# Norm sums and inverse norms of the next batch: fp32 matmuls replaced by sums of three bf16 parts

## Chip, cores, metric

One core of one Trainium2 chip. The metric is the device time of one execution in microseconds (us), the median of several. A ratio always compares with runs of the kernel before on the same chip and in the same rounds, whose medians lay between 823.33 and 823.57 us in the experiments. In a profile PE is TensorE (PEld its weight loads), DVE VectorE, ACT ScalarE, POOL GpSimd.

## The reference

Two stages: cross-covariance attention in four batches, then a gated feed-forward block over all rows.

```python
qn = q / (np.linalg.norm(q, axis=1, keepdims=True) + 1e-06)      # q, k, v: 4 x 6016 x 256
kn = k / (np.linalg.norm(k, axis=1, keepdims=True) + 1e-06)
s = kn.transpose(0, 2, 1) @ qn / tau                             # 256 x 256 per batch
a = softmax(s)                                                   # over the last axis (written out in the original)
x = v @ a
out = (silu(x @ w_gate) * (x @ w_val)) @ w_out                   # d_ff = 1536
```

## The kernel before

It never forms x. For each batch it multiplies the softmax into the two weight matrices (here Wg and Wv), then streams the values in chunks of up to 512 rows, 12 steps a chunk, 144 steps a batch. A step is two matmuls into `g_ps`, two into `v_ps`, four into `o_new` for the chunk before. While the chunks of batch b run, a plan slips the norms, logits, softmax and weight products of batch b+1 between the steps. The first batch has its own code. The change touches the plan and the norm part:

```python
def gv_step(b, ci, f, sv):                    # one step; psum_gv has two buffers per tag
    ...
    nc.scalar.activation(silu[:, :mv], g_ps[:, :mv], ACT.Silu)
    nc.vector.tensor_mul(sv[:, f, :mv], silu[:, :mv], v_ps[:, :mv])     # frees v_ps

def norm_acc(b, t):                           # squares of one pair of row groups
    ...
    for which in range(2):
        nc.scalar.activation(sq[:, :pm, which, :], ..., ACT.Square)
    ...
    for s in range(pm):
        nc.vector.tensor_add(acc, acc, sq[:, s, :, :])

def norm_cols(b):                             # sums over partitions, one column per 128 channels
    for n in range(2 * CH):
        w, h = divmod(n, CH)
        nc.tensor.matmul(cs[:, n:n + 1], acc[:, w, h * P:(h + 1) * P],
                         ones_f[:, 0:1], start=True, stop=True)          # fp32
    ...                                       # inv = 1 / (sqrt + 1e-6), on GpSimd

def norm_diag(b):
    for h in range(CH):
        nc.vector.tensor_scalar_mul(diag[:, h, :], in0=identf, scalar1=inv[:, CH + h:CH + h + 1])

def norm_rows(b):                             # inverse norms of k along the free axis
    nc.tensor.matmul(ps, ones_f, state[b, "diag"], start=True, stop=True)   # fp32
    nc.vector.tensor_copy(ink, ps)

# OutStage: at every sixth step half of an output chunk is copied out of PSUM,
# by ScalarE at steps 5, 17, 29, ... of a batch, by VectorE at 11, 23, 35, ...

LOAD0, SQ0 = 10, 22
for t in range(NP):                           # NP = 24 pairs
    step = SQ0 + (5 * t) // 2
    plan[step].append((norm_acc, t))
    plan[step + 1].append((gemm1_pair, t))
S1 = SQ0 + (5 * NP) // 2 + 1
plan[S1].append((norm_cols,))
plan[S1 + 6].append((norm_diag,))
plan[S1 + 7].append((norm_rows,))
...
```

Of the kernel before, what the change touches and what calls it, by code (L numbers as in the profile page):

```python
# [8 lines left out]
FP32 = mybir.dt.float32  # L9
BF16 = mybir.dt.bfloat16  # L10
FP8 = mybir.dt.float8e5
ALU = mybir.AluOpType
# [5 lines left out]
def kernel(  # L18
# [11 lines left out]
    nc = tc.nc  # L30
    P = 128

    B, N, C = q.shape
    D, DFF = moe_w_gate.shape
    assert C == D and C == 2 * P
    CH = C // P
# [24 lines left out]
    work = ctx.enter_context(tc.tile_pool(name="work", bufs=2))  # L61
# [13 lines left out]
    ones_bf = const.tile([P, P], BF16)  # L75
    ones_f = const.tile([P, P], FP32)
# [4 lines left out]
    identf = const.tile([P, P], FP32)  # L81
    ident = const.tile([P, P], BF16)
# [11 lines left out]
    state = {}  # L94
# [174 lines left out]
    def norm_acc(b, t):  # L269
# [12 lines left out]
        for s in range(pm):  # L282
            nc.vector.tensor_add(acc, acc, sq[:, s, :, :])  # L283

    def norm_cols(b):

        acc = state[b, "acc"]
        cs = psum_m.tile([P, 2 * CH], FP32, tag="misc")
        for n in range(2 * CH):
            w, h = divmod(n, CH)  # L290
            nc.tensor.matmul(cs[:, n:n + 1], acc[:, w, h * P:(h + 1) * P],  # L291
                             ones_f[:, 0:1], start=True, stop=True)
        inv = work.tile([P, 2 * CH], FP32, tag="inv")
        nc.vector.tensor_copy(inv, cs)  # L294
        nc.gpsimd.tensor_tensor(out=inv, in0=inv, in1=half, op=ALU.pow)  # L295
        nc.gpsimd.tensor_scalar_add(inv, in0=inv, scalar1=1e-6)
        nc.gpsimd.tensor_tensor(out=inv, in0=inv, in1=minus, op=ALU.pow)
        state[b, "inv"] = inv

    def norm_diag(b):  # L300
        inv = state[b, "inv"]
        diag = work.tile([P, CH, P], FP32, tag="diag")
        for h in range(CH):
            nc.vector.tensor_scalar_mul(diag[:, h, :], in0=identf,
                                        scalar1=inv[:, CH + h:CH + h + 1])
        state[b, "diag"] = diag

    def norm_rows(b):
        ps = psum_m.tile([P, C], FP32, tag="misc")
        nc.tensor.matmul(ps, ones_f, state[b, "diag"], start=True, stop=True)  # L310
        ink = work.tile([P, C], FP32, tag="ink")
        nc.vector.tensor_copy(ink, ps)
        state[b, "ink"] = ink
# [130 lines left out]
                    nc.sync.dma_start(out=self.dst[:, j0:j0 + m, :], in_=o_sb[:, :m, :])  # L444


    LOAD0, SQ0 = 10, 22
    plan = [[] for _ in range(STEPS)]
    for g in range(len(groups)):
        plan[LOAD0 + 5 * g].append((load_qk, g, 0))  # L450
# [1 line left out]
    for t in range(NP):  # L452
        step = SQ0 + (5 * t) // 2
        plan[step].append((norm_acc, t))
        plan[step + 1].append((gemm1_pair, t))
    S1 = SQ0 + (5 * NP) // 2 + 1
    plan[S1].append((norm_cols,))
    plan[S1 + 6].append((norm_diag,))
    plan[S1 + 7].append((norm_rows,))
    plan[S1 + 9].append((logits, 0))  # L460
    plan[S1 + 10].append((logits, 1))
    plan[S1 + 11].append((half_tanh,))
    for n in range(4):
        plan[S1 + 14 + n].append((recip, n))
    plan[S1 + 18].append((exponentials,))
    plan[S1 + 20].append((row_sums,))
    for u in range(len(wp_units)):
        plan[S1 + 22 + (u * 3) // 2].append((wp_unit, u))

    def background(b, step):  # L470
        for what, *args in plan[step]:
# [108 lines left out]
```

## Time and profile before

| | before |
|---|---|
| median time, us (5 rounds) | 823.41 (823.39 to 823.59) |
| span of the profiled run, us | 821.8 |
| TensorE busy, share of the span | 97% |
| chain that ended last, share on TensorE | 92% |
| GpSimd busy, us | 90.1 |

The reading goes from the chain (TensorE sets the end) to the timeline of TensorE, where the price of an inserted block is the distance between the `g_ps` starts around it, beyond the 1.30 us of a plain step. Every step time in this document is such a distance. The prediction below shows those lines. One caution on busy time: this trace has 4937 matmul records where the one after has 5039, because some are missing (weight loads: 5024 and 5039, and the change adds 15).

### The profile page before, as it was taken

What the parts mean: (1) busy time and instruction counts of PE and PEld (TensorE: products, weight loads), DVE (VectorE), ACT (ScalarE), POOL (GpSimd) and SP (SyncE); (2) the same over time, 40 slices, a digit from 0 to 9 for tenths busy, and PEclk for the clock granted to TensorE, in tenths of its full rate; (3) what the DMA queues carried; (4) which work ended last, traced back from release to release, by engine and by line L of the source; (5) the groups of instructions that cost most, each with busy time, mean ns of one, the idle gap of its engine ahead of it and who ended that gap; (6) DMA issues with size and microseconds to landing.
All of it is one profiled execution on the core that took longest, in us unless ns stands there. A gap on an engine that the chain in (4) does not pass through costs nothing.

```text
span 821.8 us, 13520 instructions
## 1 busy us (share of the span) xinstructions
PE 800.2 (97%) x4937; PEld 489.6 (60%) x5024; DVE 552.4 (67%) x870; ACT 461.8 (56%) x826; POOL 90.1 (11%) x171
## 2 busy tenths in 40 slices
PE   7799999999999999999999999999999999999998
PEld 4556566665665566565565656666556565666656
DVE  5576888675655888867556688877665555555554
ACT  2566777555445677645545677755544544544543
POOL 5433000133200000024300000013000000000000
PEclk9999999999999999999999999999999999999999
DMA  9999912169942121129991111125912112112101
GB/s 88 145 160 134 135 39 65 39 119 140 144 90 46 39 65 45 47 52 147 143 150 52 46 52 39 40 65 107 166 39 65 45 40 65 52 39 65 49 26 58
DMA packets 92673, 64.57 MB, mean 79 GB/s; under 512 B 52560, under 2 KB 91472, under 8 KB 91856
## 3 DMA queue, kind: packets, MB, share of 16 engines
q0 software_dynamic: 18656, 27.01, 26.0%
q1 hardware_dynamic: 73952, 36.71, 18.4%
q8 instruction: 39, 0.64, 0.3%
q14 instruction: 26, 0.21, 0.1%
HBM read 78.64 MB, written 36.70 MB: 140 GB/s over the span
## 4 chain that ended last, share of the span: by engine, by line
PE 92%; DMA 3%; ACT 2%; DVE 2%; issue 1%; POOL 0%; DVEq 0%; ACTq 0%; POOLq 0%
PE o_new L432 30%; PE v_ps L404 29%; PE g_ps L404 28%; DMA q_sb<-in_q_dram 2%; PE ps L373 2%; PE kq_new L149 2%; ACT sq L274 1%; DVE sv L408 1%; DMA k_sb<-in_k_dram 1%; DVE acc_new L283 1%; PE cs L291 0%; PE ss_new L176 0%; ACT sq L166 0%; ACT silu L407 0%; PE unit_ps L373 0%
## 5 line engine op out<-in xcount | busy, mean ns | idle before, releaser
L408 DVE TENSOR_TENSOR sv<-silu,v_ps 128x512 bf16<-128x512 bf16 (+1 forms) x576 | 382.6, 673 | 220.1 <-ACT silu L407 218.9
L407 ACT ACTIVATE silu<-g_ps 128x512 bf16<-128x512 f32 (+1 forms) x576 | 337.5, 587 | 305.2 <-PE g_ps L404 252.1
L432 PE MATMUL o_new<-w_out_sb,sv 128*128 128x256 bf16 x2256 | 338.4, 273 | 1.5
L404 PE MATMUL v_ps<-vT,Wv 128*128 128x512 bf16 (+1 forms) x1100 | 324.3, 374 | 6.2 <-DVE sv L408 3.5
L404 PE MATMUL g_ps<-vT,Wg 128*128 128x512 bf16 (+1 forms) x1075 | 319.7, 375 | 0.2
L432 PEld LDWEIGHTS <-sv 128*128 128x128 bf16 x2256 | 220.7, 98 | 140.8
L404 PEld LDWEIGHTS <-Wv 128*128 128x128 bf16 x1152 | 112.7, 98 | 135.0 <-issue 5.4
L404 PEld LDWEIGHTS <-Wg 128*128 128x128 bf16 x1152 | 107.1, 98 | 27.6 <-issue 0.2
L283 DVE TENSOR_TENSOR acc_new<-acc_new,sq 128x512 f32<-128x512 f32 x135 | 93.3, 691 | 23.6 <-ACT sq L274 21.2
L274 ACT ACTIVATE sq<-q_sb 128x512 bf16<-128x512 fp8e5 x72 | 44.3, 615 | 0.0
L274 ACT ACTIVATE sq<-k_sb 128x512 bf16<-128x512 fp8e5 x72 | 44.1, 612 | 0.0
L149 PE MATMUL kq_new<-k_sb,q_sb 128*128 128x512 fp8e5 x184 | 43.3, 317 | 0.3 <-DMA k_sb<-in_k_dram 0.3
L295 POOL TENSOR_TENSOR inv<-inv,half 128x4 f32<-128x4 f32 x3 | 3.1, 1035 | 343.9 <-DVE inv L294 343.9
L441 ACT COPY o_sb<-o_new 128x512 f32<-128x512 f32 x48 | 28.1, 585 | 14.0 <-PE o_new L432 13.7
L443 DVE COPY o_sb<-o_new 128x512 f32<-128x512 f32 (+1 forms) x48 | 31.8, 662 | 3.0 <-PE o_new L432 3.0
L104 POOL DMA_DIRECT2D q_sb<-in_q_dram x48 | 26.1, 544 | 40.1 <-DMA q_sb<-in_q_dram 15.1
L104 POOL DMA_DIRECT2D k_sb<-in_k_dram x48 | 25.9, 540 | 39.5 <-DMA q_sb<-in_q_dram 20.8
L112 POOL DMA_DIRECT2D vb<-in_v_dram x47 | 23.6, 505 | 23.3 <-DMA k_sb<-in_k_dram 14.2
L176 PE MATMUL ss_new<-sq,ones_bf 128*128 128x256 bf16 x91 | 18.3, 285 | 7.5 <-DVE sq L163 6.2
L163 DVE TENSOR_TENSOR sq<-k_sb 128x512 bf16<-128x512 fp8e5 (+1 forms) x24 | 15.2, 681 | 14.2 <-DMA k_sb<-in_k_dram 12.5
L166 ACT ACTIVATE sq<-q_sb 128x512 bf16<-128x512 fp8e5 x23 | 13.0, 619 | 20.1 <-DMA q_sb<-in_q_dram 16.6
L149 PEld LDWEIGHTS <-q_sb 128*128 128x256 fp8e5 x184 | 23.1, 140 | 2.0 <-DMA q_sb<-in_q_dram 0.8
(79 smaller groups left out, 164.5 us busy)
## 6 DMA issues: line engine op xcount, KB each, us to landing
out_dram<-o_sb SPq DMA_DIRECT2D x92, 256.0 KB, 2.4
vb<-in_v_dram POOLq DMA_DIRECT2D x43, 256.0 KB, 10.7
k_sb<-in_k_dram POOLq DMA_DIRECT2D x44, 128.0 KB, 11.6
q_sb<-in_q_dram POOLq DMA_DIRECT2D x44, 128.0 KB, 11.8
w_gate_sb<-in_moe_w_gate_dram POOLq DMA_DIRECT2D x3, 256.0 KB, 9.5
w_val_sb<-in_moe_w_val_dram POOLq DMA_DIRECT2D x3, 256.0 KB, 9.6
w_out_sb<-in_moe_w_out_dram POOLq DMA_DIRECT2D x1, 768.0 KB, 14.3
vb<-in_v_dram POOLq DMA_DIRECT2D x4, 192.0 KB, 4.5
```

Source lines behind the costliest of these rows:

```text
L104: nc.gpsimd.dma_start(out=dst[:, gs:gs + gm, :], in_=src[b].rearrange("(p s) c -> p s c", s=NS)[:, gs:gs + gm, :])
L112: nc.gpsimd.dma_start(out=vb[:mv, :].rearrange("(p s) c -> p (s c)", s=cm), in_=v[b, cs * P:cs * P + mv, :].rearrange("(p s) c -> p (s c)" ...
L149: nc.tensor.matmul(kq[:, jh, :], q_sb[:, ps:ps + 2, js], k_sb[:, ps:ps + 2, :], start=(t == 0 and jh == 0), stop=last, perf_mode=DR, skip_ ...
L176: nc.tensor.matmul(state[b, "ss", which], ones_bf, sq[:, s, :], start=(t == 0 and s == 0), stop=(t == t_last and s == pm - 1))
L274: nc.scalar.activation(sq[:, :pm, which, :], qk_tiles[b][which][:, ps:ps + pm, :], ACT.Square)
L283: nc.vector.tensor_add(acc, acc, sq[:, s, :, :])
L404: nc.tensor.matmul(dst[:, :mv], W[:, kk, fs], vT[:, kk, :mv], start=(kk == 0), stop=(kk == CH - 1))
L407: nc.scalar.activation(silu[:, :mv], g_ps[:, :mv], ACT.Silu)
L408: nc.vector.tensor_mul(sv[:, f, :mv], silu[:, :mv], v_ps[:, :mv])
L432: nc.tensor.matmul(self.o_ps[:, j % 2, :], self.sv[:, f, j * P:(j + 1) * P], w_out_sb[:, f, :], start=(f == 0), stop=(f == FH - 1))
L441: nc.scalar.copy(o_sb[:, :m, :], self.o_ps[:, :m, :])
L443: nc.vector.tensor_copy(o_sb[:, :m, :], self.o_ps[:, :m, :])
```

## The change

Intent: no fp32 matmul beside the chunks. A float32 is cut into three bf16 parts whose sum is meant to be exact, the cutting goes to GpSimd, which is mostly idle (11% busy before), and TensorE multiplies the three parts in bf16 and adds them in PSUM. To give GpSimd time, everything behind the squares moves away from them by 10 to 15 steps, and loads and squares move one step earlier, so that on the batch's own count the former are 9 to 14 steps later.

```diff
+    def split3(src, shape, tag):
+        ...
+        nc.gpsimd.tensor_copy(hi, src)
+        nc.gpsimd.tensor_tensor(out=rest, in0=src, in1=hi, op=ALU.subtract)
+        nc.gpsimd.tensor_copy(mid, rest)
+        nc.gpsimd.tensor_tensor(out=lo, in0=rest, in1=mid, op=ALU.subtract)
+        return hi, mid, lo
+
+    def norm_split(b):
+        state[b, "acc3"] = split3(state[b, "acc"], [P, 2, C], "acc")
     def norm_cols(b):
-            nc.tensor.matmul(cs[:, n:n + 1], acc[:, w, h * P:(h + 1) * P],
-                             ones_f[:, 0:1], start=True, stop=True)
+            for i, part in enumerate(state[b, "acc3"]):
+                nc.tensor.matmul(cs[:, n:n + 1], part[:, w, h * P:(h + 1) * P],
+                                 ones_bf[:, 0:1], start=(i == 0), stop=(i == 2))
...
+        parts = split3(inv[:, CH:], [P, CH], "ink")
+        for i, part in enumerate(parts):
+            nc.gpsimd.tensor_copy(scal[:, i, :], part)
     def norm_diag(b):
+        for i in range(3):
+            for h in range(CH):
+                nc.vector.tensor_scalar_mul(diag[:, i, h, :], in0=ident, scalar1=scal[:, i, h:h + 1])
     def norm_rows(b):
-        nc.tensor.matmul(ps, ones_f, state[b, "diag"], start=True, stop=True)
+        for i in range(3):
+            nc.tensor.matmul(ps, ones_bf, state[b, "diag"][:, i], start=(i == 0), stop=(i == 2))
...
-    LOAD0, SQ0 = 10, 22
+    LOAD0, SQ0 = 9, 21
-    plan[S1].append((norm_cols,))
-    plan[S1 + 6].append((norm_diag,))
-    plan[S1 + 7].append((norm_rows,))
+    plan[S1].append((norm_split,))
+    plan[S1 + 10].append((norm_cols,))
+    plan[S1 + 20].append((norm_diag,))
+    plan[S1 + 22].append((norm_rows,))
...                                          # logits to row sums 15 steps later, weight products 14
```

More of the change, by code (lines that the diff above doesn't have):

```diff
@@ L283, in norm_acc @@
             nc.vector.tensor_add(acc, acc, sq[:, s, :, :])
+    def split3(src, shape, tag):
+        hi = work.tile(shape, BF16, tag=tag + "_hi")
+        mid = work.tile(shape, BF16, tag=tag + "_mid")
+        lo = work.tile(shape, BF16, tag=tag + "_lo")
+        rest = work.tile(shape, FP32, tag=tag + "_rest")
+        nc.gpsimd.tensor_copy(hi, src)
[5 more added lines that the diff above has]
+        state[b, "acc3"] = split3(state[b, "acc"], [P, 2, C], "acc")
     def norm_cols(b):
-        acc = state[b, "acc"]
         cs = psum_m.tile([P, 2 * CH], FP32, tag="misc")
@@ L298, in norm_cols @@
         state[b, "inv"] = inv
-    def norm_diag(b):
-        inv = state[b, "inv"]
-        diag = work.tile([P, CH, P], FP32, tag="diag")
-        for h in range(CH):
-            nc.vector.tensor_scalar_mul(diag[:, h, :], in0=identf,
-                                        scalar1=inv[:, CH + h:CH + h + 1])
+        parts = split3(inv[:, CH:], [P, CH], "ink")
+        scal = work.tile([P, 3, CH], FP32, tag="scal")
+        for i, part in enumerate(parts):
+            nc.gpsimd.tensor_copy(scal[:, i, :], part)
+        state[b, "scal"] = scal
+    def norm_diag(b):
+        scal = state[b, "scal"]
+        diag = work.tile([P, 3, CH, P], BF16, tag="diag")
+        for i in range(3):
+            for h in range(CH):
+                nc.vector.tensor_scalar_mul(diag[:, i, h, :], in0=ident,
+                                            scalar1=scal[:, i, h:h + 1])
         state[b, "diag"] = diag
@@ L309, in norm_rows @@
         ps = psum_m.tile([P, C], FP32, tag="misc")
-        nc.tensor.matmul(ps, ones_f, state[b, "diag"], start=True, stop=True)
+        for i in range(3):
+            nc.tensor.matmul(ps, ones_bf, state[b, "diag"][:, i], start=(i == 0),
+                             stop=(i == 2))
         ink = work.tile([P, C], FP32, tag="ink")
@@ L456 @@
     S1 = SQ0 + (5 * NP) // 2 + 1
-    plan[S1].append((norm_cols,))
-    plan[S1 + 6].append((norm_diag,))
-    plan[S1 + 7].append((norm_rows,))
-    plan[S1 + 9].append((logits, 0))
-    plan[S1 + 10].append((logits, 1))
-    plan[S1 + 11].append((half_tanh,))
+    plan[S1].append((norm_split,))
+    plan[S1 + 10].append((norm_cols,))
+    plan[S1 + 20].append((norm_diag,))
+    plan[S1 + 22].append((norm_rows,))
+    plan[S1 + 24].append((logits, 0))
+    plan[S1 + 25].append((logits, 1))
+    plan[S1 + 26].append((half_tanh,))
     for n in range(4):
-        plan[S1 + 14 + n].append((recip, n))
-    plan[S1 + 18].append((exponentials,))
-    plan[S1 + 20].append((row_sums,))
+        plan[S1 + 29 + n].append((recip, n))
+    plan[S1 + 33].append((exponentials,))
+    plan[S1 + 35].append((row_sums,))
     for u in range(len(wp_units)):
-        plan[S1 + 22 + (u * 3) // 2].append((wp_unit, u))
+        plan[S1 + 36 + (u * 3) // 2].append((wp_unit, u))
     def background(b, step):
```

## The prediction

Its prices are those of the trace before.

> **What bounds the kernel now.** I read four views of the kernel before, in this order: the totals and the slices on the page, the chain that ended last, the waits of TensorE, and then the timeline around the instructions that the change touches.
>
> The totals and the chain say which engine sets the end.
>
> ```profile
> PE 800.2 (97%) x4937; PEld 489.6 (60%) x5024; DVE 552.4 (67%) x870; ACT 461.8 (56%) x826; POOL 90.1 (11%) x171
> ...
> PEclk9999999999999999999999999999999999999999
> ...
> PE 92%; DMA 3%; ACT 2%; DVE 2%; issue 1%; POOL 0%; DVEq 0%; ACTq 0%; POOLq 0%
> ```
>
> TensorE is busy 97% of 821.8 us at full granted clock and is 92% of the chain; GpSimd is busy 11% and absent from the chain. So whatever leaves TensorE's stream shortens the run one for one, and whatever is added to GpSimd costs only if somebody comes to wait for it. Busy records of TensorE overlap, so I don't take savings from them; I take them from the distance between starts. The stream is a row of equal steps (two matmuls into g_ps, two into v_ps, four into o_new), and a step takes 1.30 us from the start of g_ps to the next start of g_ps. What is in between beyond 1.30 us is the price of the extra work.
>
> The timeline of TensorE at the norm sums of the second batch:
>
> ```profile
> 154.18 0.59 PE L404 MATMUL g_ps<-vT,Wg 128*128 128x512 bf16 x2
> 154.61 0.59 PE L404 MATMUL v_ps<-vT,Wv 128*128 128x512 bf16 x2
> 155.04 0.60 PE L432 MATMUL o_new<-w_out_sb,sv 128*128 128x256 bf16 x4
> 155.48 0.95 PE L291 MATMUL cs<-ones_f,acc_new 128*128 128x1 f32 x8
> 156.29 0.59 PE L404 MATMUL g_ps<-vT,Wg 128*128 128x512 bf16 x2
> ```
>
> The fp32 block stands in the stream from 155.48 to 156.29: 0.81 us for 8 records (4 matmuls, two records each), 0.10 us each.
>
> The rows of inverse norms, the same batch:
>
> ```profile
> 165.39 0.60 PE L310 MATMUL ps<-diag,ones_f 128*128 128x256 f32 x2
> 165.82 0.38 PE L404 MATMUL g_ps<-vT,Wg 128*128 128x512 bf16 x1
> ```
>
> One fp32 matmul of 256 columns holds the stream for 0.43 us (165.39 to 165.82). A bf16 one of 256 columns takes 0.108 us (four of o_new in 0.44 us above).
>
> And the model for what replaces them, the row sums of the exponentials, which are bf16 with one moving column:
>
> ```profile
> 182.72 0.24 PE L351 MATMUL rs<-ones_bf,exT 128*128 128x1 bf16 x4
> 182.83 0.38 PE L404 MATMUL g_ps<-vT,Wg 128*128 128x512 bf16 x1
> ```
>
> Four of them, each with its own weight load, hold the stream for 0.11 us, 0.027 us each.
>
> Last, the waits of TensorE inside the steps:
>
> ```profile
> PE v_ps L404 <- DVE sv L408: 3.5, 6, 0.7
> ```
>
> Six times, twice a batch, TensorE waits for VectorE to release v_ps. I return to these, because the change moves them.
>
> [...]0.43 us is four times the 0.108 us of bf16 at the same width.[...]while GpSimd wrote den (171.56 to 172.17), the sv product that began at 170.98 still took 0.69 us. [...]the trace has one-input at 128x512 fp32, den, 0.61 us. It has no two-input one of that size.
>
> **The change part by part.** It applies to three of the four batches; the first has its own code.
>
> (1) Norm sums. Removed: 8 fp32 records, 0.81 us. Added: 4 columns x 3 parts = 12 bf16 matmuls x 0.027 = 0.32 us. On the path: -0.49 us.
>
> (2) Rows of inverse norms. Removed 0.43 us, added 3 x 0.108 = 0.32 us. On the path: -0.11 us.
>
> (3) GpSimd, split of the sums: two copies (about 0.6 us each, from den) and two subtractions[...]. The plan leaves ten steps, 13 us, between the split and its first matmul, and the last add of the squares ends two to three steps ahead of the split. Off the path: 0.
>
> (4) GpSimd, inverse norms: the three old operations (1.03 + 0.22 + 1.04 us) and seven tiny ones, about 0.25 us each by the 0.22 us of the 128x4 add of a scalar: some 4 us against ten steps again. Off the path: 0.
>
> (5) VectorE: six diagonal products in place of two. Two fp32 ones took 0.48 us together, 0.24 each; six are at most 1.4 us in one step, where VectorE has 1.30 - 0.69 = 0.6 us free. The lag of 0.8 us is below what TensorE tolerates: sv of one step is finished about 1.1 us before the matmuls two steps on want its v_ps buffer (sv ends 156.13; the second next v_ps starts at 157.2 if nothing is inserted). The four reciprocals of 0.94 us already make a larger lag (4 x (0.69 + 0.94 - 1.30) = 1.3 us, over four steps) and there every step stays at 1.30 us. Off the path: 0.
>
> (6) Loads. GpSimd also issues them, in program order. The den operation, which holds the queue until the tanh is done, comes 14 steps (18 us) later, so the next values and the next q and k go out at about 190 us, not 172. The value chunk behind it is wanted two chunks (24 steps) later, and the next squares at step 21 of the next batch. Off the path: 0.
>
> (7) The squares move one step earlier (step 21, not 22, of the batch). That is not neutral in itself. The copy of an output half on ScalarE falls on steps 5, 17, 29, 41, 53, 65, 77, and each time a pair of squares is issued in the same step, ScalarE has 0.58 + 2 x 0.62 us of extra work, the adds come late on VectorE, and v_ps is released late three steps on. In the kernel before the squares fall on 22, 24, 27, 29, 32, ...: steps 29 and 77 coincide. The two step times that are long are indeed those three steps later: 1.97 us in place of 1.30 and 2.19 in place of 1.52 (0.22 of extra matmuls), 0.67 each. Now the squares fall on 21, 23, 26, ..., 41, 43, ..., 53, 56, ...: steps 41 and 53 coincide. Again two, so I keep 2 x 0.67. The VectorE copies (steps 11, 23, 35, 47, 59, 71) coincide with squares at 47 and 59 before, of which only 59, preceded by squares two steps earlier, cost 0.09 us. Now they coincide at 23 and 71: 23 comes behind the first pair, which has one add rather than two, and 71 has three steps in front of it as 47 had. So -0.09 us.
>
> (8) The tail of the softmax and the twelve weight products run 13 to 15 steps later and end at step 134 of 144. They cost the same 0.43 us per unit; two of their VectorE evacuations now meet an output copy, but steps there are 1.73 us long. 0, with ten steps in hand.
>
> Sum per batch: -0.49 - 0.11 - 0.09 = -0.69 us; three batches: -2.1 us. 823.4 - 2.1 = 821.3 us, 0.25%.
>
> **The rivals.** (a) A worse coincidence: step 41 is followed by a full pair of squares two steps later, where step 77 before was followed by the half-size last pair. I worked the queue through: sv would end at about 153.0 on the old time axis against a need at about 153.3, so no second wait, but the margin is 0.3 us. If it fails, up to 0.7 us a batch: about 823 us. (b) Weight loads bind: the first of the four row-sum loads is prefetched, and twelve in a row could settle at the 0.05 us that I would read if the loads' own 0.10 us records overlapped only two deep. Then (1) saves 0.81 - 0.65 = 0.16 us and the total is about 822.3 us. Against it: the last three of the four loads start within 0.08 us. (c) GpSimd becomes a wait: splits held by VectorE or much slower than I think. It would need over 9 us on the split to reach TensorE. Then 1 us for each us beyond, three times: 824 us or more. The 11% share and the idle 343.9 us in front of its inv operation speak against it. (d) The late q and k loads collide with something: the q and k of a batch have some 55 us to arrive; before, steps kept 1.30 us while loads ran. 0.
>
> **Range and chances.** The times of before agree within 0.04 us, so the range is about the terms: low end if both coincidences get milder by another 0.1 us a batch, 820.6; high end with (a) or (b), 822.8. Two per cent is 16.5 us, far beyond the whole block removed (1.24 x 3 = 3.7 us) on one side and anything I found on the other: within 2% at 0.985, faster 0.005, slower 0.01.
>
> **What would show it.** The norm-sum matmuls holding the stream for 0.3 us (not 0.65); the rows for 0.32; the v_ps wait for sv still about 3.5 us in total with six long times, now three steps after 41 and 53; no wait of TensorE for the parts or for diag[...]. The prediction is wrong if step times outside these places change, or if VectorE's sv product lengthens beside the splits.

## The result, and the profile after

| | before | after |
|---|---|---|
| median time, us (5 rounds) | 823.41 | 821.51 (821.17 to 821.78) |
| span of the profiled run, us | 821.8 | 819.5 |
| norm sums: stream of TensorE held, us | 0.81 | 0.31 |
| rows: stream held, us | 0.43 | 0.32 |
| steps long beyond their matmuls, us per batch | 1.42 | 1.42 |
| GpSimd busy, us | 90.1 | 104.7 |

The ratio is 0.9976, 95% interval 0.9962 to 0.9991: inside 2%, and faster. The outputs are right. A ratio is the mean time of one kernel's runs over that of the other's of the same rounds, so not quite the ratio of the medians quoted.

The page's totals and chain after, the same lines as before:

```profile
PE 804.1 (98%) x5039; PEld 488.2 (60%) x5039; DVE 552.9 (67%) x882; ACT 462.1 (56%) x826; POOL 104.7 (13%) x204
...
PEclk9999999999999999999999999999999999999999
...
PE 92%; DMA 2%; DVE 2%; ACT 2%; issue 1%; POOL 1%; DVEq 0%; ACTq 0%; POOLq 0%
```

TensorE still sets the end, at full clock (1.00 in every stretch from 42 to 800 us, before and after). GpSimd's 1% in the chain is mostly load issues ahead of the first step (4.0 us, all before 6.2 us of the span), not the cutting.

The timeline of TensorE after, at the norm sums of the second batch, which run beside the chunks of the first. The columns are start and length in us, engine, line, operation, operands; eight of the twelve rows are left out.

```profile
166.35 0.60 PE L456 MATMUL o_new<-w_out_sb,sv 128*128 128x256 bf16 x4
166.78 0.17 PE L307 MATMUL cs<-ones_bf,hi 128*128 128x1 bf16 x1
166.81 0.16 PE L307 MATMUL cs<-ones_bf,mid 128*128 128x1 bf16 x1
166.84 0.16 PE L307 MATMUL cs<-ones_bf,lo 128*128 128x1 bf16 x1
...
167.06 0.16 PE L307 MATMUL cs<-ones_bf,lo 128*128 128x1 bf16 x1
167.09 0.38 PE L428 MATMUL g_ps<-vT,Wg 128*128 128x512 bf16 x1
```

Twelve matmuls start 0.025 us apart, and `g_ps` starts 0.31 us after the first of them. A record is 0.16 us long and its neighbours overlap it: the distance is the price, not the length. The rows, in the same view:

```profile
182.69 0.49 PE L333 MATMUL ps<-diag,ones_bf 128*128 128x256 bf16 x3
183.01 0.59 PE L428 MATMUL g_ps<-vT,Wg 128*128 128x512 bf16 x2
```

GpSimd's timeline shows where the cutting went:

```profile
149.81 0.61 POOL L292 CAST hi<-acc_new 128x512 bf16<-128x512 f32 x1 [65.49 <-DVE acc_new L283]
150.50 1.15 POOL L293 TENSOR_TENSOR rest<-acc_new,hi 128x512 f32<-128x512 f32 x1
151.72 0.61 POOL L294 CAST mid<-rest 128x512 bf16<-128x512 f32 x1
152.41 1.16 POOL L295 TENSOR_TENSOR lo<-rest,mid 128x512 bf16<-128x512 f32 x1
```

It sat idle for 65 us (the bracket), started when the last add was done, and ended at 153.57, thirteen us before TensorE used the parts. (Only its place in GpSimd's program is set by the plan's step for the cutting; it began as soon as the adds allowed.)

Where the span went: the distance from step 12 to the end of each of the first three batches, those that carry a next batch's work, fell by 0.62 us each, 1.87 us together. The fourth is equal to 0.01 us. The remaining 0.39 us of the 2.26 us between the two profiled spans lies before the first step, whose first weight load began at 40.80 us before and 40.41 after. The change has nothing there; in all the profiles that start lies between 40.04 and 40.80 us. Two waits for the first loads (9.7 and 10.6 us) make up 20 of those 40 us on the chain after, so I take it for their scatter, which no run tests. Whatever its cause, profiled spans here differ by some tenths without a reason in the steps.

The waits of TensorE after, the answer to the line of 3.5 us before:

```profile
PE v_ps L428 <- DVE sv L432: 3.0, 6, 0.5
```

Six times again, and the long steps are now 44 and 56 of each batch: 2.19 us where its matmuls need 1.52, and 1.97 where they need 1.30, 0.67 each. (The 3.0 against 3.5 us is no gain: the step times show the full 0.67 us. Other profiles of the same plan show 3.5.) A third is short, 0.08 us at step 51. How such a step comes about is in the timelines of three engines around step 44. ScalarE, four rows:

```profile
94.68 0.60 ACT L431 ACTIVATE silu<-g_ps 128x512 bf16<-128x512 f32 x1 [0.70 <-PE g_ps L428]
95.55 0.58 ACT L465 COPY o_sb<-o_new 128x512 f32<-128x512 f32 x1 [0.27 <-PE o_new L456]
96.03 0.63 ACT L274 ACTIVATE sq<-q_sb 128x512 bf16<-128x512 fp8e5 x1
96.56 0.62 ACT L274 ACTIVATE sq<-k_sb 128x512 bf16<-128x512 fp8e5 x1
```

VectorE, three rows:

```profile
95.31 0.69 DVE L432 TENSOR_TENSOR sv<-silu,v_ps 128x512 bf16<-128x512 bf16 x1 [0.49 <-ACT silu L431]
97.22 1.42 DVE L283 TENSOR_TENSOR acc_new<-acc_new,sq 128x512 f32<-128x512 f32 x2 [1.21 <-ACT sq L274]
98.55 1.28 DVE L432 TENSOR_TENSOR sv<-silu,v_ps 128x512 bf16<-128x512 bf16 x2
```

TensorE:

```profile
98.19 0.59 PE L428 MATMUL g_ps<-vT,Wg 128*128 128x512 bf16 x2
99.28 0.59 PE L428 MATMUL v_ps<-vT,Wv 128*128 128x512 bf16 x2 [0.50 <-DVE sv L432]
```

The copy of the output half goes first on ScalarE, so the squares end at 97.18 us. VectorE, which takes its instructions in program order in this timeline, idles 1.21 us, then does the two adds (from 97.22 us), and only then, at 98.55, the product that frees a `v_ps` buffer. TensorE reaches that buffer at step 44 and waits 0.50 us.

### The profile page after: what moved, and what is told of

The parts are those of the page before. It is cut to its first block, busy times and chain, and to the rows that moved or that the text cites. A ratio compares the mean times of both kernels' runs of the same rounds, so it can differ in the third digit from the quotient of the medians.

```text
span 819.5 us, 13681 instructions
## 1 busy us (share of the span) xinstructions
PE 804.1 (98%) x5039; PEld 488.2 (60%) x5039; DVE 552.9 (67%) x882; ACT 462.1 (56%) x826; POOL 104.7 (13%) x204
## 4 chain that ended last, share of the span: by engine, by line
PE 92%; DMA 2%; DVE 2%; ACT 2%; issue 1%; POOL 1%; DVEq 0%; ACTq 0%; POOLq 0%
PE o_new L456 29%; PE v_ps L428 29%; PE g_ps L428 29%; DMA q_sb<-in_q_dram 2%; PE ps L397 2%; PE kq_new L149 2%; DVE sv L432 1%; ACT sq L274 1%; DVE acc_new L283 1%; POOL k_sb L104 0%; PE ss_new L176 0%; ACT sq L166 0%; ACT silu L431 0%; PE unit_ps L397 0%; POOL q_sb L104 0%
## 5 line engine op out<-in xcount | busy, mean ns | idle before, releaser
L428 PE MATMUL v_ps<-vT,Wv 128*128 128x512 bf16 (+1 forms) x1128 | 330.4, 374 | 3.0 <-DVE sv L432 3.0
L428 PE MATMUL g_ps<-vT,Wg 128*128 128x512 bf16 (+1 forms) x1128 | 331.1, 375 | 0.0
L292 POOL CAST hi<-acc_new 128x512 bf16<-128x512 f32 x3 | 1.8, 605 | 294.3 <-DVE acc_new L283 294.3
```

The lines of the kernel that those rows point to most:

```text
L428: nc.tensor.matmul(dst[:, :mv], W[:, kk, fs], vT[:, kk, :mv], start=(kk == 0), stop=(kk == CH - 1))
```

## The experiments

Eleven kernels ran; all gave correct results. My theory: the gain is the shorter time that the matmuls hold TensorE's stream and nothing else, GpSimd's work is hidden by the plan's slack, and the shift of the squares is neutral. The rival: the plan, not the bf16 parts, carries the gain (or hides a cost). Each kernel was profiled. A batch is named by its chunks, so the third batch carries the norms of the fourth.

**The plan alone.** The kernel before with the new distances, fp32 kept.

```diff
-    LOAD0, SQ0 = 10, 22
+    LOAD0, SQ0 = 9, 21
-    plan[S1].append((norm_cols,))
+    plan[S1 + 10].append((norm_cols,))
...                                          # and so on, without norm_split
```

> The kernel before with the changed kernel's plan alone (loads and squares one step earlier, the norm and softmax work later), fp32 matmuls kept. Theory ([...]the plan is neutral): within 0.3 us of the kernel before, the steps that are long by 0.67 us move from 32 and 80 to 44 and 56 and the 0.09 us from 62 to 51, the two fp32 blocks still 0.81 and 0.43 us. Rival (the plan carries the gain): about 821.5 us, 1.9 us faster.

Measured: 823.65 us against 823.33, ratio 1.0002 (0.999 to 1.0015). The long steps sat at 44, 56 and 51 and the fp32 blocks held the stream 0.81 and 0.43 us. The interval is wide, about 1 us to either side, and the step times decide: the first two batches took what they took in the kernel before, within 0.01 us. One step of the third batch (74) was 0.2 us longer, here and in one other profile. The timeline of VectorE shows how: three steps before, where its output copy and a pair of squares meet at step 71, its product began 1.50 us after the step's `g_ps` in place of 1.26, with ScalarE no later than elsewhere, and copy and adds came behind it. Why it began late stays open. The plan carries no gain. The rival falls.

**Squares back.** The changed kernel with the squares where they were.

```diff
-    LOAD0, SQ0 = 9, 21
+    LOAD0, SQ0 = 10, 22
-    S1 = SQ0 + (5 * NP) // 2 + 1
+    S1 = SQ0 + (5 * NP) // 2
```

> The changed kernel with loads and squares back at steps 10 and 22, everything after the squares where the changed kernel has it. Theory: the same time as the changed kernel within 0.3 us (about 821.5), with the long steps again at 32, 62 and 80. Rival (the earlier squares matter): back toward 823.4 us, or a stall total per batch other than 1.43 us.

Measured: 821.43 us, ratio 0.9976, as the changed kernel's. Long steps at 32, 62 and 80, and every batch sum within 0.02 us of the changed kernel's. The shift by one step is neutral, because it trades two coincidences for two others.

**Rows in fp32 again.** Only `norm_diag` and `norm_rows` of the kernel before put back into the changed kernel.

```diff
-        for i in range(3):
-            nc.tensor.matmul(ps, ones_bf, state[b, "diag"][:, i], start=(i == 0), stop=(i == 2))
+        nc.tensor.matmul(ps, ones_f, state[b, "diag"], start=True, stop=True)
```

> The changed kernel with the rows of inverse norms by the old fp32 matmul again. Theory: the block of the rows holds TensorE's stream 0.43 us rather than 0.33, so 0.3 us slower than the changed kernel in three batches, about 821.8; the rest of the steps as in the changed kernel. Rival (the loads of ones, three in place of two, or the six diagonal products eat it): no difference, or a gain.

Measured: 822.05 us; 0.11 us more per batch at step 104, and the 0.2 us at step 74 of the third batch again. 0.11 x 3 is the 0.3 us expected.

**Sums in fp32 again.** Only the matmuls of `norm_cols` put back; GpSimd still cuts, and nobody reads the parts.

```diff
-            for i, part in enumerate(state[b, "acc3"]):
-                nc.tensor.matmul(cs[:, n:n + 1], part[:, w, h * P:(h + 1) * P], ones_bf[:, 0:1], ...)
+            nc.tensor.matmul(cs[:, n:n + 1], state[b, "acc"][:, w, h * P:(h + 1) * P], ones_f[:, 0:1], ...)
```

> The changed kernel with the norm sums by the old fp32 matmuls again, the split left on GpSimd unused. Theory: the block holds 0.81 us rather than 0.30, so 1.5 us slower than the changed kernel, about 823.0. Rival (GpSimd's split costs something by itself): slower than 823.4 us, or VectorE's products longer than 0.69 us beside the split.

Measured: 822.87 us. Each batch is 0.51 us longer than in the changed kernel, all of it at step 92: 1.53 us. The two parts add up to the whole: 0.51 + 0.11 = 0.62. Against the kernel before each batch is still 0.11 us shorter, the share of the rows, and VectorE's products beside the cutting took 0.68 to 0.69 us: the cutting itself cost TensorE nothing here.

**The slack of the cutting taken away.**

```diff
-    plan[S1].append((norm_split,))
-    plan[S1 + 10].append((norm_cols,))
+    plan[S1 - 3].append((norm_split,))
+    plan[S1 - 2].append((norm_cols,))
```

> The changed kernel with the slack of the split taken away: split right behind the last squares, its matmuls right behind the last q-k product (step 80). In the changed kernel the split ends at 153.57 us and the matmuls would be wanted at 151.19. Theory (GpSimd's 3.7 us are hidden by the slack alone): TensorE waits about 2.4 us per batch for the last part, 7.2 us in all, about 828.7 us. Rival (the split isn't on any path even then, or is much faster): 821.5 us.

Measured: 830.21 us, 1.5 us more than expected. TensorE's timeline at the norm sums of the second batch, the first matmul of each part:

```profile
150.82 0.17 PE L307 MATMUL cs<-ones_bf,hi 128*128 128x1 bf16 x1
152.03 0.18 PE L307 MATMUL cs<-ones_bf,mid 128*128 128x1 bf16 x1 [1.05 <-POOL mid L294]
153.27 0.18 PE L307 MATMUL cs<-ones_bf,lo 128*128 128x1 bf16 x1 [1.06 <-POOL lo L295]
```

It waits for the second part, then for the third; step 80 is 2.7 us longer, of which 0.3 are the matmuls that moved there: 2.4 us of waiting (2.5 in the third batch), as expected. In the third batch the three steps behind that block were longer by another 1.68 us, which nobody had expected, and this view by stretch shows a lower granted clock there (columns: stretch, length, busy time and count of each engine, then granted clock, DMA share, GB/s):

```profile
546.00:551.00 5.00, 2.82 (x29) 1.87 (x28) 1.97 (x4) 1.13 (x2) 3.52 (x4) 1.00 0.06 19
551.00:555.00 4.00, 3.95 (x18) 2.03 (x17) 1.41 (x3) 1.19 (x2) 3.20 (x9) 0.62 0.00 0
```

After the wait the mean granted clock was 0.62 for 4 us and 0.96 for the next 5. If it stood at half, as it did in the long row below (0.50), that makes 3.4 us of it, an estimate from these means. The three batches are 2.41, 2.42 and 4.17 us longer than in the changed kernel, 9.0 together; the first step of this profile began 0.37 us earlier, and the spans differ by 8.6 us, the medians by 8.7. So GpSimd's cutting is not cheap. It is hidden; without the slack the waits alone cost 7.3 us, nearly four times what the change gains.

**The old distances.** How much of the new slack is needed?

```diff
-    plan[S1].append((norm_split,))
-    plan[S1 + 10].append((norm_cols,))
-    plan[S1 + 20].append((norm_diag,))
-    plan[S1 + 22].append((norm_rows,))
+    plan[S1 - 3].append((norm_split,))
+    plan[S1].append((norm_cols,))
+    plan[S1 + 6].append((norm_diag,))
+    plan[S1 + 7].append((norm_rows,))
...
```

> The changed kernel with the old distances: split right behind the last squares (step 79), norm sums at the old step and everything behind it at the old distances, 10 to 15 steps earlier than in the changed kernel. Theory: the split ends 0.2 us before its matmuls are wanted and the inverse norms about 2 us before the diagonal products, so no wait and the same 821.5 us within 0.3. Rival (the longer distances are needed): one more wait of TensorE per batch, of 0.5 us or more, at the sums or the rows.

Measured: 821.79 us, 0.3 more than the changed kernel; the step times say 0.16 to 0.17 per batch, 0.5 in all. The sums kept their 0.31 us, with 0.2 us to spare: the cutting ended at 153.74 and its first matmul started at 153.94. The rows held the stream 0.49 us in place of 0.32: VectorE's six diagonal products, from 162.61 to 163.67 us, ended after the third matmul was wanted (0.11 us behind the second, at 163.56), because rows followed diagonals by one step, not two. So of the ten to fifteen added steps one is worth 0.16 us per batch, and the rest are reserve in this run.

**The price of one matmul, multiplied.** The twelve matmuls 21 times over, then 6 times.

```diff
-        for n in range(2 * CH):
+        for n in [n for _ in range(21) for n in range(2 * CH)]:
```

> The changed kernel with the twelve bf16 matmuls of the norm sums issued 21 times over (same result). Theory: 20 further times 0.30 us in three batches, 18 us, about 839.5 us, from the 0.025 us that one takes between starts in the trace. Rival (weight loads bind in a long row, 0.05 us each): 36 us, about 858 us.

Measured: 846.72 us, 25.2 us more than the changed kernel and not 18. Step 92 is longer by 6.13 to 6.14 us, 0.0255 us each over the 240 more matmuls, close to the theory's 20 x 0.30. The rest, 2.3 to 2.4 us per batch, came in the two steps behind:

```profile
core 0: us, PE busy (x) PEld busy (x) DVE busy (x) ACT busy (x) POOL busy (x), PEclk, DMA share, GB/s
166.40:172.80 6.40, 6.40 (x251) 6.39 (x249) 0.69 (x1) 0.01 (x1) 0.00 (x0) 0.84 0.02 5
172.80:177.50 4.70, 4.48 (x23) 2.18 (x22) 0.89 (x3) 1.19 (x2) 3.66 (x11) 0.50 0.00 0
```

TensorE had no gap in its records for 6.4 us (busy 6.40 of 6.40), and the granted clock then stood at half, for about 6.8 us from inside the row on (an estimate from 0.84 over 6.40 us and 0.50 over 4.70). The whole run's mean clock was 0.986. Neither of my theories had that. At the end of the row, by that estimate at half the clock, the one-column matmuls still started 0.027 us apart (172.26 to 172.90 us). In both cases of a fallen clock the fall and the longer steps stand together in the trace; what in TensorE's work makes the clock fall, no run separates. The shorter row was to tell whether the clock makes the new matmuls dearer than their 0.31 us:

> The changed kernel with the twelve bf16 matmuls of the norm sums issued 6 times over. At 21 times over, the row stood 6.2 us in the stream, as 0.025 us each make it, but the granted clock then fell to half for 6.8 us, which cost 2.4 us more per batch. Theory (price 0.025 us each[...]): 5 x 0.30 us x 3 = 4.5 us, about 826.0 us, clock undisturbed. Rival (any longer row of one-column matmuls lowers the clock): 1.5 to 2.4 us more per batch, 830 to 833 us.

Measured: 826.03 us; step 92 at 3.10 us, so 1.50 us for 60 more matmuls, 0.025 each. The steps behind the row took 1.30 us in each batch, and the mean granted clock was 0.996 to 1.0 in the four runs: six times the changed kernel's twelve left the clock alone. Side by side: the clock fell with a row of 252 in 6.4 us without a gap, and in one batch of three with 2.5 us of waiting amid a row of twelve; with a row of 72, 1.8 us, it did not.

**The coincidences taken away.** The traces pointed to a cost that the change only moved, so I moved the squares off the copies.

```diff
-        step = SQ0 + (5 * t) // 2
+        step = SQ0 + (5 * t) // 2 + {8: -1, 13: 1}.get(t, 0)
```

> The changed kernel with the two pairs of squares that fall on the step of a ScalarE output copy moved by one step (pair 8 from step 41 to 40, pair 13 from 53 to 54). Theory (the coincidence of copy and squares makes VectorE release v_ps late): the steps long by 0.67 us vanish, 1.34 us per batch, 4.0 us in all, about 817.5 us; the wait of TensorE for sv falls from 3.0 us to under 0.5. Rival (the stall belongs to the squares' density, not to the copy): it moves to neighbouring steps and the time stays at 821.5 us.

Measured: 817.38 us, ratio 0.9924 (0.9912 to 0.9937). Each of the three batches is 1.32 to 1.33 us shorter than in the changed kernel. ScalarE around the same copy now:

```profile
93.82 0.62 ACT L274 ACTIVATE sq<-q_sb 128x512 bf16<-128x512 fp8e5 x1
94.34 0.62 ACT L274 ACTIVATE sq<-k_sb 128x512 bf16<-128x512 fp8e5 x1
94.86 0.59 ACT L431 ACTIVATE silu<-g_ps 128x512 bf16<-128x512 f32 x1
95.49 0.59 ACT L465 COPY o_sb<-o_new 128x512 f32<-128x512 f32 x1
```

The squares are done before the copy, and TensorE's list of waits has no entry for `v_ps` any more. The 0.08 us at step 51 stayed. There the VectorE copy of step 47 stands between pairs at 46 and 48, so pair 10 moved too:

```diff
+        step = SQ0 + (5 * t) // 2 + {8: -1, 10: -1, 13: 1}.get(t, 0)
```

> The kernel with pairs 8 and 13 moved, and pair 10 moved too (step 46 to 45), so that the VectorE output copy of step 47 doesn't stand between two pairs one step away. Theory: the 0.08 us at step 51 vanishes as well, 0.25 us in three batches, about 817.1 us, and no step of the squares is longer than its matmuls. Rival (it comes from the density of the squares alone): 817.4 us, the 0.08 us at another step.

Measured: 817.02 us, ratio 0.9922 (0.991 to 0.9935); the 0.08 us are gone from the step times, and no step of the squares exceeds its matmuls. This is the best version that I ran: 6.5 us under the kernel before, of which the change proper is 1.9. And the same lever on the kernel before, without the change:

```diff
-        step = SQ0 + (5 * t) // 2
+        step = SQ0 + (5 * t) // 2 + {3: 1, 22: -1}.get(t, 0)
```

> The kernel before, fp32 matmuls and its plan kept, with the two pairs of squares that meet a ScalarE output copy moved by one step (pair 3 from 29 to 30, pair 22 from 77 to 76). Theory (the copy's coincidence is a cost of its own, independent of the change): 1.34 us per batch less, 4.0 us in all, about 819.4 us. Rival (moving them only helps with the changed kernel's plan): 823.4 us.

Measured: 819.57 us against 823.57, ratio 0.9953. Its two long steps are gone (step 80 takes the 1.52 us that its matmuls need); the 0.08 us at step 62, which I left alone, is there. The lever is independent of the change, and worth twice as much.

## Why the prediction was right

The time was 821.51 us against 821.3, and the sum is right for its own reasons, with one term wrong. The medians' difference of 1.90 us agrees with the 1.87 us that the steps give, so the first loads' scatter did not help it.

- Step (1), norm sums, -0.49 us: measured 0.81 to 0.31. Undoing it alone cost 0.51. Rival (b), weight loads that bind, fell: 0.025 us each in a row of 12 and of 72, and 0.0255 on average for the 240 added in the row of 252. (Its 0.65 us was a slip: twelve at 0.05 make 0.60.)
- Step (2), rows, -0.11 us: measured 0.43 to 0.32, and 0.11 when undone. The ratio of the two types is not the same at one column: an fp32 matmul with its weight loads took 0.20 us of the stream there (0.81 us for four), a bf16 one 0.025, a factor of eight, where 256 columns gave four (0.43 us against 0.108). In the trace before, the two weight loads of each one-column fp32 matmul are 0.19 us long and start 0.11 us apart, and so do its matmul records from the second on (bf16 loads are 0.10 us long); whether the loads set the price, no run here separates.
- Steps (3) and (4), GpSimd off the path: cutting took 3.76 us, the inverse norms' chain 3.9 against 4, and neither was waited for. VectorE's `sv` product beside the cutting stayed at 0.69 us. The prediction's own line for that was weak, since the product that began at 170.98 lay beside `den` for only 0.11 us; in the run after, one that began at 152.45 lies wholly within the second subtraction. Rival (c)'s bound of 9 us is low as well: from the last add to the first matmul on the parts TensorE left 17 us. Rival (c) is true only where the slack is taken away. GpSimd's busy time rose by 14.6 us (90.1 to 104.7); a subtraction took 1.15 us, a copy 0.61, and a tiny operation 0.19 rather than 0.25.
- Step (5), six diagonal products: 1.06 us against at most 1.4, no wait. With rows one step behind them they do cost 0.16 us.
- Steps (6) and (8), loads and the later tail: the next values went out at 189.89 us (172.13 before), as worked out, and nobody came to wait; the fourth batch, which carries no next batch's work, is unchanged, and the three others differ only at the sums, the rows and the moved steps.
- Step (7), squares: the two long steps came three steps after 41 and 53, 0.67 us each, as worked out, and rival (a), a second wait behind step 41, did not come. The term of -0.09 us is the one that failed: VectorE's copies were to cost nothing any more, and they cost what they had cost before. The old 0.09 us did vanish from step 62, but the same, 0.085 us, came at step 51, which by the prediction's own sign (a step time outside the named places changes) is a miss. I had looked only at squares in the very step of a VectorE copy; a copy between two pairs that stand one step away on either side, at 46 and 48, does the same. Moving pair 10 removed it. So the sum per batch is -0.62, not -0.69, and -1.87 us in all. The high end of the range, 822.8, did not cover rival (a) in full either: 0.7 us a batch would have made 823.4.

## What to carry to other kernels

In a stream that one engine binds, take prices from the distance between starts, not from record lengths (here 0.025 us against records of 0.16), and for the shape at hand. The prices at 256 columns (0.43 us in fp32, 0.108 in bf16) give the gain of the rows, 0.32 us for 0.43, but not that of the sums, 0.31 for 0.81, which is the larger. Here three bf16 parts beat fp32 by 1.9 us with thirteen us of slack for the 3.76 us of cutting, and lost by 6.7 us without it (830.21 against 823.55), so the slack is part of the price. When a change shifts a periodic job against other periodic jobs, list the steps where they meet on one engine before and after, including neighbours. Here the meetings were worth twice the change, on either kernel.
